# V^T by one transposing DMA in place of TensorE transposes, in the backward pass of attention over a cache

## The chip, the core and the metric

The kernel runs on one core of one Trainium2 chip. The metric is the device time of one execution in microseconds. Three runs of the kernel before gave 5222.84, 5231.35 and 5238.27 us; the median is 5231.35 us.

## What is computed

Forward and backward of a block with two branches on a layer-normalised input xn (2048 rows, 576 columns, bf16): attention with 32 heads of 128 over a K and a V cache of 2048 rows, and a gated branch of width 4608. The output is x + s * silu(B), and the gradients go to x, both caches and all weights.

```
def _A_ref(x, k_cache, v_cache, wq, wo):          # s
    q = (x @ wq) -> [B, H, Sq, Dh]
    scores = einsum("bhqd,bhkd->bhqk", q, k_cache) * Dh ** -0.5
    p = softmax(scores)
    o = einsum("bhqk,bhkd->bhqd", p, v_cache)
    return o.transpose.reshape(B, Sq, H * Dh) @ wo
def _B_ref(x, w_gate, w_up, w_down):
    h = sigmoid(x @ w_gate) * (x @ w_up)
    return h @ w_down
out = x + _A_ref(xn, ...) * silu(_B_ref(xn, ...))
_out, _vjp = jax.vjp(_f, A_x, A_k_cache, A_v_cache, A_wq, A_wo, B_w_gate, B_w_up, B_w_down)
return (_out, *_vjp(grad_out))
```

The backward pass of attention needs, per head, dP = dO V^T. With the head's dimension on the partitions, both factors of this product have to lie in memory as [128 of the head, 2048 rows]; so V, which is loaded in its natural form, has to be transposed once per head.

## The kernel before

The gated branch comes first (lines 165 to 327), then attention (lines 330 to 657), then the weight gradients and the gradient of x (from line 659). The change lies in the attention stage alone.

Attention goes head by head. One head has two halves. In the P half, for each of 16 tiles of 128 query rows, TensorE makes scores (`s_half`, L465), VectorE scales them and tracks the extreme value (L467), and ScalarE takes the exponential of the whole row block, which gives Pq, 128 x 2048 in bf16 (`s_exp`, L476). In the dS half, for each of the same tiles, TensorE makes dP from dO^T and V^T (`dp_half`, L495), and VectorE, with ScalarE's help, turns it into dSq, again 128 x 2048 (L498, L501, L505). Each Pq and nearly each dSq is transposed by a DMA of its own, issued on the SyncE queue (`trans_dma`, L513), into a tile PT or dST; there are 7 such tiles. The dSq of query tile 9 alone is transposed on TensorE, by 16 transposes into PSUM and two copies (`trans_pe`). TensorE then uses PT and V for the output rows and dST and K for dQ (`row_mm`, L525), and Pq with dO and dSq with Q for the gradients of V and K (`kv_mm`, L544).

The tiles K^T, dO by rows, V^T and Q by rows are made with TensorE too: `pe_transposes` (L428 to L432) does 8 transposes into one PSUM accumulator and one copy out of it, and is called twice for each of these tiles. For V^T this is `prep_vt` (L439 to L442): 16 transposes of the natural V tile `Vn`, and two copies on VectorE (L42) into `VT`. Both tiles exist once (`ld1`, one buffer). `load_kv` loads `Kn` and `Vn` on the GpSimd queue, for the next head while the current one runs.

The order of the work is written out by hand. A head is 64 positions long: the P half takes positions 0 to 32 of the head, the dS half 32 to 64. `at(pos, ...)` puts a piece of work at a position; scores and dP are anchors at fixed positions, and everything is emitted in the order of positions. Under `tc.manual_schedule(engines=MAN)` the engines in `MAN` (TensorE, VectorE, ScalarE) execute in exactly this order, while the instructions of SyncE and GpSimd are placed by the scheduler of the framework. The positions that matter here: PT of query tile qt at 2 qt + 2.7, dST at 32 + 2 qt + 2.0, the first use of a group of four PT or dST some 9.4 positions after the first of them, V^T at 22.2 and 24.2. In the last head five loads of output weights (`load_wo`, L374) are written at positions 50 to 62; they fill space that was taken by xnT and dsT and are used in the stage that follows attention.

Of the kernel before, what the change touches and what calls it, by code (L numbers as in the profile page):

```python
# [9 lines left out]
bf = mybir.dt.bfloat16  # L10
# [3 lines left out]
P = 128  # L14
# [81 lines left out]
def kernel(  # L96
# [6 lines left out]
    nc = tc.nc  # L103
    cfg = dict(cfg or {})
    _, S, D = A_x.shape
# [232 lines left out]
    with tc.tile_pool(name="ld2", bufs=2) as ld2, tc.tile_pool(name="ld1q", bufs=1) as ld1q, \  # L338
# [17 lines left out]
        def at(pos, fn, *args):  # L356
            prog.append((pos, len(prog), fn, args))

        def anchor(pos, fn, *args):
            anchors.append((pos, len(anchors), fn, args))  # L360
# [67 lines left out]
        def pe_transposes(src_fn, dst, g, eng):  # L428
            pt = ps_acc.tile([P, 8, P], bf, name="acct", tag="acc")
            for j in range(8):  # L430
                nc.tensor.transpose(pt[:, j, :], src_fn(g * 8 + j), ident[:])  # L431
            alt.copy(dst[:, g * 8:(g + 1) * 8, :], pt[:], eng=eng)  # L432
# [3 lines left out]
                hs.KT = ld1.tile([P, S], bf, name="KT")  # L436
            pe_transposes(lambda j: hs.Kn[:, j, :], hs.KT[:].rearrange("p (t q) -> p t q", q=P), g, eng)

        def prep_vt(hs, g, eng):  # L439
            if g == 0:  # L440
                hs.VT = ld1.tile([P, S], bf, name="VT")
            pe_transposes(lambda j: hs.Vn[:, j, :], hs.VT[:].rearrange("p (t q) -> p t q", q=P), g, eng)  # L442

        def prep_don(hs, g, eng):
            if g == 0:
# [84 lines left out]
        def rows(pos, step, width, hs, T, rhs, g, sinks):  # L530
            bx = Box()
            sink, after = sinks
            for j in range(GQ):
                for kt in range(NT):
                    at(pos + step * j + width * kt / NT, row_mm, bx, hs, T, rhs, g * GQ + j, kt, sink)
            if after:
                at(pos + step * (GQ - 1) + width + AFTER, after)
# [11 lines left out]
        def kv(pos, end, hs, slabs, rhs, half, out_dram):  # L549
            ov = out_dram.rearrange("(p t) d -> p t d", t=NT)  # L550
            bx = Box()
            bx.acc = [None, None]

            def sink(acc, i):
                c = half * 2 + i
                kv_t = stg.tile([P, KPC, P], bf, name="kv")
                alt.copy(kv_t[:], acc[:], eng=KVE[i])
                nc.gpsimd.dma_start(ov[:, c * KPC:(c + 1) * KPC, :], kv_t[:])

            n = 2 * KPC  # L560
            for qt in range(NT):
                for j in range(n):
                    at(pos + (end - pos) * (qt * n + j) / (NT * n), kv_mm, bx, hs, slabs, rhs, half, qt, j, sink)

        def o_sink(hs, g):
            gs = slice(g * GQ, (g + 1) * GQ)
            bx = Box()

            def sink(acc):
                bx.ou = wt.tile([P, GQ, P], bf, name="ou")  # L570
                alt.copy(bx.ou[:], acc[:], eng=OUE)
                bx.prod = wt.tile([P, GQ, P], f32, name="prod", bufs=1)
                nc.gpsimd.tensor_tensor(bx.prod[:], bx.ou[:], hs.dOn[:, gs, :], op=ALU.mult)

            def after():
                prod, ou = bx.prod, bx.ou
                o_n = stg.tile([P, GQ, P], bf, name="o_n", bufs=1)
                nc.vector.tensor_reduce(hs.delta[:, gs], prod[:], axis=AX.X, op=ALU.add)
                nc.gpsimd.tensor_scalar(hs.negdelta[:, gs], hs.delta[:, gs], -1.0, None, op0=ALU.mult)
                nc.gpsimd.tensor_tensor(o_n[:], ou[:], bcast(hs.rinv_all[:, gs], GQ), op=ALU.mult)  # L580
                nc.gpsimd.dma_start(on2_d[g * CH:(g + 1) * CH, hs.h * P:(hs.h + 1) * P].rearrange("(t p) d -> p t d", p=P), o_n[:])

            return sink, after

        def dq_sink(hs, g):
            gs = slice(g * GQ, (g + 1) * GQ)

            def sink(acc):
                dq_n = stg.tile([P, GQ, P], bf, name="dq_n")
                nc.vector.tensor_tensor(dq_n[:], acc[:], bcast(hs.rsc[:, gs], GQ), op=ALU.mult)  # L590
                nc.gpsimd.dma_start(dq2_d[g * CH:(g + 1) * CH, hs.h * P:(hs.h + 1) * P].rearrange("(t p) d -> p t d", p=P), dq_n[:])  # L591

            return sink, None
# [3 lines left out]
        XO, XQ = 12.1, 12.1  # L597
        VA, VB, KA, KB = (22, 38.0), (38.5, 53.5), (58.0, 69.5), (70.5, 82.0)
        QP, DO, KVE, PJE, OUE = (41.0, 3.0), (4.0, 2.5), "ss", "sv", "s"
        KT_AT, DON_AT, VT_AT, QN_AT = (46.3, 2, "v"), (7.2, 5, "v"), (22.2, 2, "v"), (38.3, 2, "s")  # L600
        EXP_AT, RINV_AT, PT_AT, DST_AT, AFTER = 2.1, 4.6, 2.7, 2.0, 3.5
        WO_AT = 50.0
        MAN = {mybir.EngineType.PE, mybir.EngineType.DVE, mybir.EngineType.Activation}
        for h in range(H):
            hs = Head(h)
            b = h * HEAD
            back = lambda x: b - HEAD + x if h else b - 14 + x / 8
            at(back(35.0), load_w, hs)
            at(back(35.1), load_kv, hs)
            for c in range(NCH):  # L610
                at(back(QP[0] + QP[1] * c), proj, hs, "QT", c, PJE[0])
                at(b + DO[0] + DO[1] * c, proj, hs, "dOT", c, PJE[1])
            at(b + DO[0] - 2, prep_wo, hs, "s")
            for g in range(2):
                at(back(KT_AT[0] + KT_AT[1] * g), prep_kt, hs, g, KT_AT[2])
                at(b + DON_AT[0] + DON_AT[1] * g, prep_don, hs, g, DON_AT[2])
                at(b + VT_AT[0] + VT_AT[1] * g, prep_vt, hs, g, VT_AT[2])
                at(b + QN_AT[0] + QN_AT[1] * g, prep_qn, hs, g, QN_AT[2])
            for p in range(NT // 2):
                at(b + 4 * p + 2 + RINV_AT, s_rinv, hs, p)  # L620
                at(b + max(4 * p + 2.1 + RINV_AT, DON_AT[0] + DON_AT[1] * (p // 4) + 0.5), s_scale, hs, p)
            for qt in range(NT):
                p1, p2 = b + 2 * qt, b + H1 + 2 * qt
                for hf in range(NHF):
                    anchor(p1 + hf, s_half, hs, qt, hf)
                    anchor(p2 + hf, dp_half, hs, qt, hf)
                at(p1 + EXP_AT, s_exp, hs, qt)
                if qt in PE_P:
                    for g in range(2):
                        at(p1 + 5.3 + g, trans_pe, hs.PT, hs.P, qt, "PT", g, "s")  # L630
                else:
                    at(p1 + PT_AT, trans_dma, hs.PT, hs.P, qt, "PT")
                if qt in PE_DS:
                    for g in range(2):
                        at(p2 + 4.3 + g, trans_pe, hs.dST, hs.dS, qt, "dST", g, "sv"[g])
                else:
                    at(p2 + DST_AT, trans_dma, hs.dST, hs.dS, qt, "dST")
            for g in range(NG):
                rows(b + 8 * g + XO, 2, 2, hs, hs.PT, "Vn", g, o_sink(hs, g))
                rows(b + H1 + 8 * g + XQ, 2, 2, hs, hs.dST, "Kn", g, dq_sink(hs, g))  # L640
            for half, (pv, pk_) in enumerate(((VA, KA), (VB, KB))):
                kv(b + pv[0], b + pv[1], hs, hs.P, "dOn", half, out_3[0, h])
                kv(b + pk_[0], b + pk_[1], hs, hs.dS, "Qn", half, out_2[0, h])
# [4 lines left out]
                at(bl + WO_AT + 3 * k, load_wo, h0, min(h1, H - 1))  # L648
        prog.sort(key=lambda e: e[:2])
        anchors.sort(key=lambda e: e[:2])  # L650
        with tc.manual_schedule(engines=MAN):
            nxt = 0
            for (pos, _, fn, args) in prog:
                while nxt < len(anchors) and anchors[nxt][0] <= pos:
                    anchors[nxt][2](*anchors[nxt][3])
                    nxt += 1
                fn(*args)

    OB = 5
    if True:  # L660
# [19 lines left out]
        with tc.tile_pool(name="c1b", bufs=1, side="right", reuse_waits="tile") as blk, \  # L680
# [3 lines left out]
                tc.tile_pool(name="c1pt", bufs=2, space=PSUM) as pst, \  # L684
                tc.manual_schedule(engines=MAN | {mybir.EngineType.SP, mybir.EngineType.Pool}):
            gins = {}
# [188 lines left out]
        with tc.tile_pool(name="c4c", bufs=1, reuse_waits="tile") as chp, tc.tile_pool(name="c4s", bufs=2, reuse_waits="tile") as sb, \  # L875
# [10 lines left out]
            for sbi in range(S // SB2):  # L886
# [20 lines left out]
                for sl in range(nsl):  # L907
# [17 lines left out]
                    t = sb.tile([P, D], f32, name="t")  # L925
# [38 lines left out]
```

## Time and profile before

| what | value |
|---|---|
| median of three runs | 5231.35 us |
| span of the profiled execution | 5231.1 us |
| heads | 32, the first scores at 517.3 us, the last head from 3640.0 us |
| transposing DMAs of PT, dST | 512 and 480, median landing 5.7 and 6.2 us after the issue |
| transposes of V on TensorE | 512, median 219 ns |
| copies into VT on VectorE | 64, median 686 ns |
| bytes on SyncE's DMA queue in one head (1562.2 to 1663.4 us) | 16.85 MB |
| bytes on GpSimd's DMA queue in the same stretch | 3.44 MB |

The profile is of one execution. The profiler gives the span from the first to the last instruction, and no other time of that execution; the span is 0.25 us below the median of the runs. Busy times are per engine; TensorE's matmuls overlap each other, so that the busy time of a group is less than the count times the mean. The granted TensorE clock is full in every head. SyncE only issues DMAs, so its rows show the length of the issuing instruction, which includes the wait for a semaphore and for a place in the queue. In a row of the waits the name in front waited, and the name behind the arrow ended the wait.

### The profile page before, as it was taken

The page shows a single profiled execution, that of the slowest core. Times are in us where ns is not written, and L with a number is a line of the kernel's source. Part 1 is how long each engine was busy: PE and PEld are TensorE (multiplying, and loading weights), DVE is VectorE, ACT ScalarE, POOL GpSimd, SP SyncE. Part 2 cuts the span into 40 slices and gives each one's busy share as a digit, 9 for nine tenths or more (in the row PEclk, how much of TensorE's full clock was granted, in tenths as well). Part 3 has the DMA queues.
Part 4 walks back from the last instruction along what each step waited for, and adds up shares of the span by engine and source line. Part 5 has one row for each costly group of instructions (what it writes and reads, how often), then busy time and mean ns, then how long its engine had stood idle before and what let it go on. Part 6 is the DMA issues. An engine that isn't in the chain of part 4 may idle for free.

```text
span 5231.1 us, 128038 instructions
## 1 busy us (share of the span) xinstructions
PE 5100.0 (97%) x55184; PEld 3649.0 (70%) x55184; DVE 3262.9 (62%) x5108; ACT 2290.1 (44%) x2931; POOL 1444.3 (28%) x2102
## 2 busy tenths in 40 slices
PE   8999999999999999999999999999899999999999
PEld 3444777777777777777777777777657788744454
DVE  4545888888888888888888888888532222210111
ACT  6531665565566556556556655655301221100000
POOL 2222233233233323323323332332222222211000
PEclk9999999999999999999999999999999999999999
DMA  7489999999999999999999999999999556686765
GB/s 274 183 205 166 190 192 199 193 197 194 193 197 198 198 198 199 199 197 195 197 202 198 194 201 199 197 197 201 204 223 227 174 169 185 200 232 152 162 146 124
DMA packets 2712232, 1013.46 MB, mean 194 GB/s; under 512 B 2525296, under 2 KB 2645872, under 8 KB 2711664
## 3 DMA queue, kind: packets, MB, share of 16 engines
q1 hardware_dynamic: 2628256, 726.57, 80.8%
q0 software_dynamic: 83408, 278.71, 17.9%
q8 instruction: 431, 7.06, 0.6%
q14 instruction: 137, 1.12, 0.1%
HBM read 172.54 MB, written 201.00 MB: 71 GB/s over the span
## 4 chain that ended last, share of the span: by engine, by line
PE 81%; issue 6%; DVE 6%; DMA 5%; POOL 1%; SPq 1%; ACT 0%; DVEq 0%; POOLq 0%; ACTq 0%
PE acckv L544 15%; PE acc L525 14%; PE dp L495 8%; PE acc L905 7%; PE sp L465 6%; PE accw L807 6%; DVE sneg L467 4%; PE accp L424 4%; PE dh L781 3%; PE acc L306 3%; PE accd L795 3%; PE accq L863 3%; PE acc L854 2%; PE acct L431 2%; PE acc L723 2%
## 5 line engine op out<-in xcount | busy, mean ns | idle before, releaser
L476 ACT ACTIVATE Pq<-sneg,nm 128x2048 bf16<-128x2048 bf16 x512 | 1024.5, 2001 | 389.2 <-DVE sneg L467 386.1
L525 PE MATMUL acc<-Kn,dST 128*128 128x128 bf16 x8192 | 1066.6, 219 | 22.5 <-DMA dST<-dSq 22.4
L525 PE MATMUL acc<-Vn,PT 128*128 128x128 bf16 x8192 | 1022.4, 219 | 10.7 <-DMA PT<-Pq 10.7
L544 PE MATMUL acckv<-dOn,Pq 128*128 128x128 bf16 x8192 | 1031.7, 219 | 0.0
L498 DVE SCALAR_TENSOR_TENSOR dSq<-dp,delta,Pq 128x1024 bf16<-128x1024 f32 x608 | 773.6, 1281 | 349.9 <-PE dp L495 347.6
L544 PE MATMUL acckv<-Qn,dSq 128*128 128x128 bf16 x8192 | 896.2, 219 | 0.0
L544 PEld LDWEIGHTS <-Pq 128*128 128x128 bf16 x8192 | 793.3, 98 | 117.1 <-issue 0.3
L525 PEld LDWEIGHTS <-PT 128*128 128x128 bf16 x8192 | 765.8, 98 | 153.2 <-DMA PT<-Pq 14.2
L525 PEld LDWEIGHTS <-dST 128*128 128x128 bf16 x8192 | 759.0, 98 | 158.1 <-DMA dST<-dSq 28.8
L544 PEld LDWEIGHTS <-dSq 128*128 128x128 bf16 x8192 | 719.0, 98 | 99.8 <-issue 0.3
L467 DVE TENSOR_SCALAR_CACHE_REDUCE sneg<-sp,nm 128x1024 bf16<-128x1024 f32 x512 | 656.5, 1282 | 82.0 <-PE sp L465 56.5
L467 DVE TENSOR_SCALAR_CACHE_REDUCE sneg<-sp 128x1024 bf16<-128x1024 f32 x512 | 625.0, 1221 | 59.5 <-PE sp L465 51.2
L501 ACT ACTIVATE t<-dp,negdelta 128x1024 bf16<-128x1024 f32 x416 | 463.6, 1114 | 420.1 <-PE dp L495 363.2
L465 PE MATMUL sp<-KT,QT 128*128 128x512 bf16 x2048 | 609.2, 379 | 32.5 <-DVE sneg L467 25.4
L495 PE MATMUL dp<-VT,dOT 128*128 128x512 bf16 x2048 | 609.5, 379 | 0.3 <-DVE dSq L498 0.3
L484 POOL TENSOR_TENSOR dOn<-dOn,rinv_all 128x256 bf16<-128x256 bf16 x256 | 155.9, 609 | 658.0 <-DVE rinv_all L480 540.9
L505 DVE TENSOR_TENSOR dSq<-t,Pq 128x1024 bf16<-128x1024 bf16 x416 | 319.0, 767 | 0.0
L807 PEld LDWEIGHTS <-xn_all 128*128 128x128 bf16 (+1 forms) x2880 | 282.7, 100 | 38.6 <-issue 11.1
L905 PEld LDWEIGHTS <-cf 128*128 128x128 bf16 x2304 | 146.0, 98 | 141.7 <-DMA cf<-dg_d 3.6
L918 DVE SCALAR_TENSOR_TENSOR junk<-dxn,xn_all 128x576 f32<-128x576 f32 x16 | 12.1, 758 | 370.3 <-ACT dxn L913 370.3
L591 POOL DMA_DIRECT2D dq_d<-dq_n x128 | 98.6, 770 | 471.9 <-DVE dq_n L590 463.5
L465 PEld LDWEIGHTS <-QT 128*128 128x128 bf16 x2048 | 163.3, 98 | 53.1 <-issue 51.7
(173 smaller groups left out, 6956.1 us busy)
## 6 DMA issues: line engine op xcount, KB each, us to landing
out_dram<-kv POOLq DMA_DIRECT2D x256, 128.0 KB, 4.8
h_d<-h_row POOLq DMA_DIRECT2D x48, 384.0 KB, 2.7
a_d<-a_row POOLq DMA_DIRECT2D x48, 384.0 KB, 2.6
b_d<-b_row POOLq DMA_DIRECT2D x48, 384.0 KB, 3.2
a_blk<-a_d SPq DMA_DIRECT2D x18, 1024.0 KB, 5.8
b_blk<-b_d SPq DMA_DIRECT2D x18, 1024.0 KB, 21.3
du_d<-du_blk POOLq DMA_DIRECT2D x18, 1024.0 KB, 8.5
dg_d<-dg_blk POOLq DMA_DIRECT2D x18, 1024.0 KB, 11.5
```

The costliest lines, as they stand in the source:

```text
L424: nc.tensor.matmul(acc[:], lhsT=w[:, i, :], rhs=srcT[:, i, cs], start=(i == 0), stop=False)
L465: nc.tensor.matmul(sp[:, c * CH:(c + 1) * CH], lhsT=hs.QT[:, qs], rhs=hs.KT[:, hf * HW_ + c * CH: hf * HW_ + (c + 1) * CH], start=True, st ...
L467: nc.vector.tensor_scalar(sneg[:, hf * HW_:(hf + 1) * HW_], sp[:], -SCALE, None if hf == 0 else nm[:, hf - 1:hf], op0=ALU.mult, op1=ALU.mi ...
L476: nc.scalar.activation(Pq[:], sneg[:], AF.Exp, bias=nm[:, hf:hf + 1], scale=-1.0, accum_out=hs.rs_all[:, qt:qt + 1])
L495: nc.tensor.matmul(dp[:, c * CH:(c + 1) * CH], lhsT=hs.dOT[:, qs], rhs=hs.VT[:, hf * HW_ + c * CH: hf * HW_ + (c + 1) * CH], start=True, s ...
L498: nc.vector.scalar_tensor_tensor(dSq[:, hsl], dp[:], hs.delta[:, qt:qt + 1], Pq[:, hsl], op0=ALU.subtract, op1=ALU.mult)
L501: nc.scalar.activation(t[:], dp[:], AF.Identity, bias=hs.negdelta[:, qt:qt + 1], scale=1.0)
L505: nc.vector.tensor_tensor(dSq[:, hsl], t[:], Pq[:, hsl], op=ALU.mult)
L525: nc.tensor.matmul(bx.acc[:, j, :], lhsT=T[qt][:, kt, :], rhs=getattr(hs, rhs)[:, kt, :], start=(kt == 0), stop=(kt == NT - 1))
L544: nc.tensor.matmul(bx.acc[i][:, jj, :], lhsT=slabs[qt][:, k0:k0 + P], rhs=getattr(hs, rhs)[:, qt, :], start=(qt == 0 and jj == 0), stop=(q ...
L807: nc.tensor.matmul(acc[:kd, :FB], lhsT=xn_all[:, st, d0:d0 + kd], rhs=blk_[:, st, :], start=(st == 0), stop=(st == NT - 1))
L905: nc.tensor.matmul(accs[sl][j][:, :nn], lhsT=ch[:, kk, sl * P:(sl + 1) * P], rhs=w_[:, n0:n0 + nn], start=(pi == 0 and kk == 0), stop=(las ...
```

## The change

`prep_vt`, called twice per head at positions 22.2 and 24.2, is replaced by `turn`, called once per head at position 5.6. It takes the whole `Vn` tile, 128 x 2048 in bf16, and writes `VT` by one transposing DMA on SyncE's queue. The 16 transposes on TensorE, the two PSUM accumulators and the two copies on VectorE are gone. In addition, SyncE is put among the engines that execute in the written order, for this stage. GpSimd's instructions are still placed by the scheduler.

```diff
-        def prep_vt(hs, g, eng):
-            if g == 0:
-                hs.VT = ld1.tile([P, S], bf, name="VT")
-            pe_transposes(lambda j: hs.Vn[:, j, :], hs.VT[:].rearrange("p (t q) -> p t q", q=P), g, eng)
+        def turn(hs, name, src):
+            t_ = ld1.tile([P, S], bf, name=name)
+            setattr(hs, name, t_)
+            nc.sync.dma_start_transpose(t_[:].rearrange("p (t q) -> p t q", q=P), src(hs).rearrange("p t d -> p (t d)"))
...
-        KT_AT, DON_AT, VT_AT, QN_AT = (46.3, 2, "v"), (7.2, 5, "v"), (22.2, 2, "v"), (38.3, 2, "s")
+        KT_AT, DON_AT, VT_AT, QN_AT = (46.3, 2, "v"), (7.2, 5, "v"), 5.6, (38.3, 2, "s")
...
+        MANH = MAN | {mybir.EngineType.SP}
...
+            at(b + VT_AT, turn, hs, "VT", lambda hs: hs.Vn[:])
             for g in range(2):
...
-                at(b + VT_AT[0] + VT_AT[1] * g, prep_vt, hs, g, VT_AT[2])
...
-        with tc.manual_schedule(engines=MAN):
+        with tc.manual_schedule(engines=MANH):
```

## The prediction

> **What bounds the kernel now.** The change touches only the attention stage, so I first looked for that stage on the page, in its slices and engine sums.
>
> ```profile
> PE 5100.0 (97%) x55184; PEld 3649.0 (70%) x55184; DVE 3262.9 (62%) x5108; ACT 2290.1 (44%) x2931; POOL 1444.3 (28%) x2102
> ...
> PE   8999999999999999999999999999899999999999
> ...
> DMA  7489999999999999999999999999999556686765
> ```
>
> Attention is slices 5 to 29 (the first L465 matmul starts at 517 us, the last head at 3640 us): 32 heads. TensorE and the DMA engines both stand at 9 throughout, so two resources are full together, and the change takes from one and gives to the other. The question is which one has room.
>
> TensorE first. From the matmul records, the distance between the first L465 matmuls of neighbouring heads is 100.32 us, to 0.03, in 15 of 31 heads and 100.73 us in the mean (95.5 to 105.4). A number that repeats to the hundredth is the pace of an instruction stream, not of transfers; the other heads lie above it. The waits of PE between 650 and 3600 us say why:
>
> ```profile
> PE sp L465 <- DVE sneg L467: 19.5, 58, 0.4
> PE acc L525 <- DMA dST<-dSq: 12.1, 14, 1.6
> ```
>
> (Total us, times, longest.) In 29 heads PE lost 12 us to late dS transposes. Small, but these are already arriving too late now and then. So next the SyncE queue, which issues all transposes, over two heads:
>
> ```profile
> 1538.01 52.05 SPq L513 DMA_TRANSPOSE PT<-Pq  x16
> 1590.17 48.91 SPq L513 DMA_TRANSPOSE dST<-dSq  x15
> 1639.16 50.47 SPq L513 DMA_TRANSPOSE PT<-Pq  x16
> 1689.74 50.23 SPq L513 DMA_TRANSPOSE dST<-dSq  x15
> ```
>
> (Start, length.) Each row ends within 0.12 us of the next one's start: 31 transposes fill a whole head, about 3.2 us each. Is the queue waiting for its sources, or are they waiting for it? One pair answers, the sixth dSq of that head and its transpose:
>
> ```profile
> 1600.01 0.68 DVE L505 TENSOR_TENSOR dSq<-t,Pq 128x1024 bf16<-128x1024 bf16 x1
> ...
> 1609.06 1.73 SPq L513 DMA_TRANSPOSE dST<-dSq  x1
> ```
>
> The source was done at 1600.7, its transpose was issued 8.4 us later. Doing this for every transpose of heads 2 to 30 (issue against the end of the ACT or DVE instruction that finishes its source), the sources wait 3.5 to 8 us in the dS half and 0.1 to 3.3 us in the P half; SyncE waits for a source for only 1.58 us per head, nearly all before the sixth to ninth PT. So the transpose path is occupied 100.73 - 1.58 = **99.15 us of 100.73**. PE paces most heads, with a DMA path 1.6% below its limit right behind it.
>
> **The change, part by part.**
>
> *Removed on PE:* 16 transposes per head. Their price is what they hold back on the weight-load row, not the 219 ns each on the group's line, since they overlap:
>
> ```profile
> 1567.48 0.49 PEld L431 LDWEIGHTS <-Vn 128*128 128x128 bf16 x8
> 1567.92 0.10 PEld L525 LDWEIGHTS <-PT 128*128 128x128 bf16 x1
> ```
>
> Eight take 0.44 us from start to the next start, 16 take 0.89 us, so 28 us over 32 heads. *Removed on DVE:* two copies:
>
> ```profile
> L42 DVE COPY VT<-acct 128x1024 bf16<-128x1024 bf16 x64 | 43.9, 686 | 4.7 <-PE acct L431 4.7
> ```
>
> 2 x 0.686 = 1.37 us per head. Both copies (1569.4 and 1573.0 in that head) lie in the stretch 1563 to 1575 where the chain of waits runs through L467 on DVE and PE idles, so here the copies, and not the transposes, are what the end would feel: a gain of 1.37 us per head, 44 us in all, if nothing else is late; at least the 28 us of PE. Two PSUM accumulators per head also come free; I cost that at nothing, because the one wait of PE for an accumulator in the list of waits (acct behind dq_n, 6.5 us in 29 heads) is 0.2 us per head.
>
> *Added on the DMA path:* one 128x2048 bf16 transpose per head, the same shape as PT. No row shows a VT transpose; the bounds come from its 991 sisters. Taking the landings in order, the 302 intervals in which no other queue moved anything have a lower quartile of 1.68 us and a mean of 2.08. A least-squares fit of all intervals (bytes of SyncE's queue, bytes of GpSimd's queue, instruction loads) gives 2.44 us per transpose, and with it 75 us for transposes, 11 us for GpSimd's 3.4 MB and 14 us for 11.5 instruction loads of 16 KB, together 100 us of a head. The mean occupation, 99.15 / 31 = 3.2 us, carries a share of that other traffic and is the upper end; 1.68 is the lower. I take 2.44, the fit, because the queue is backlogged where this transpose enters it. 32 fewer TensorE instruction pairs save an eighth of an instruction load, about 0.15 us.
>
> [...] The trace's 512 KB in 2.44 us are 215 GB/s, and its fast quarter 310 GB/s.
>
> *What else the new DMA does.* Position 5.6 puts it between the second and third PT. There SyncE is 3 us behind. VT is free (the last dp of the head before ended at least 13 us earlier) and Vn landed at least 37 us earlier, so the instruction adds no wait of its own; if it did, every PT behind it would be late. PT from the third on moves back by up to 2.4 us. Their reserves (landing to first use by L525, medians) are 9 us there and 2.3 to 5 us from the tenth on, and the 1.58 us of idle lies between, so the P half mostly absorbs it. The dS half inherits the rest; its reserve is 0.6 us at the eighth and 1.1 at the ninth dST. That is what will be late next.
>
> *SyncE in written order.* The transposes already issue in the written order in every head (16 PT, 15 dST), so nothing moves there. Only the five output-weight loads of L374 move: today they go out between 3630 and 3678 us, under the last head's P half, which takes 58.28 us where others take 51.40, 6.9 us lost; written, they go at positions 50 to 62, between the last dST. Their 4.57 MB are 16 to 21 us of DMA at 290 to 215 GB/s. So 6.9 us come back, and between nothing and 21 us are paid at the last dST: -7 to +14 us; I take +2, as the last dST already keep PE waiting.
>
> *Sum.* DMA per head: 99.15 + 2.44 - 0.15 = 101.44 us, plus 0.3 us of idle that remains because the reserve varies from head to head: 101.74 against 100.73, **+1.0 us**. PE would now allow 98.95 to 99.4, so its gain is not felt. Over 31 periods +31 us, with the loads +33: 5231.1 + 33 = **5264 us**. The profiled span, 5231.1, lies 0.25 us from the median of the runs, so no correction. With 1.68 us per transpose the head would be 100.7 to 101.0 (5229 to 5240); with 3.2 us, 102.5 (5231 + 55 + up to 14 = 5300).
>
> **Rivals.**
>
> *The DMA path has more room than its queue shows* (faster). A queue that is always full can hide slack: SyncE may be held only by a limit on descriptors in flight, and if the engines behind it take an extra transpose without delaying the others, PE and DVE decide, and the gain is 28 to 44 us: 5203 to 5187. For it: half the heads run at PE's exact pace in spite of the backlog. Against it: all six heads longer than 101 us (105.4 at the worst) have at most 0.8 us of SyncE idle; a path with room would not lengthen them. It decides if the marginal transpose costs under about 1 us, beneath the 5% point of 1.53 us.
>
> *A transpose costs the fast quarter or less* (no change). [...] For it: the intervals below 1.7 us. Against it: they follow a stall, when descriptors have piled up. [...]
>
> *The idle cannot be used* (slower still). If the 1.58 us lie where PT's source is late whatever the queue does, and the new DMA costs its full 3.2 us, a head costs +3.1 us: 5231 + 96 = 5327.
>
> *The change does not do what it says:* VT could be held by Vn or by the old VT. With 13 and 37 us in hand I give that nothing of its own.
>
> **Chances and range.** This kernel's measurement can tell about 0.3% (16 us) from no change. Forecast (slower, 5246 to 5300): 0.57. More room: 0.23, faster. No change: 0.16. Idle unusable: 0.04, slower. So faster 0.23, same 0.16, slower 0.61. The range reaches from the lower end of the faster rival, 5187, to the forecast's upper bound, 5300; the forecast's own is 5246 to 5300.
>
> **What would show it.** Right: the head's period no longer repeats at one value and lies near 101.7 us; PE's waits on dST grow from 12 us to over 40 us; SyncE's idle goes from 1.6 us per head towards 0.3; DVE's busy time falls by 44 us without shortening the span. Wrong: a period fixed at or below 99.4 us with dST waits as before (DMA had room), or VT's landing delayed by its own waits.

## The result and the profile after

The changed kernel is slower: 5298.39 us median (5278.81 to 5323.32, 4 runs) against 5234.81 us for the kernel before beside it, ratio 1.0112 (95% interval 1.0064 to 1.0160). On another chip with six runs of it the median was 5305.95 us and the ratio 1.0130 (1.0101 to 1.0160). The profiled execution took 5323.32 us, the longest of its four, with a span of 5321.5 us; a second profile had 5294.9 us.

The first lines of the page look almost as they did before the change; PE and the DMA engines stand at 9 again:

```profile
PE 5101.7 (96%) x54672; PEld 3627.1 (68%) x54672; DVE 3228.3 (61%) x5044; ACT 2292.4 (43%) x2931; POOL 1447.9 (27%) x2102
...
PE   8999999999999999999999999999898999999999
...
DMA  7587999999999999999999999999999665596865
```

What changed is who ends PE's waits. The waits of PE between 650 and 3600 us (total us, times, longest):

```profile
PE acc L525 <- DMA dST<-dSq: 48.3, 39, 3.3
PE acc L525 <- DMA PT<-Pq: 43.2, 53, 2.4
PE sp L465 <- DVE sneg L467: 14.3, 49, 0.7
```

dST rose from 12.1 to 48.3 us, PT from 1.7 to 43.2. Accordingly the chain that ended last now runs through transfers for 15% of the span instead of 5%. First the kernel before, then the changed one:

```profile
PE 81%; issue 6%; DVE 6%; DMA 5%; POOL 1%; SPq 1%; ACT 0%; DVEq 0%; POOLq 0%; ACTq 0%
```

```profile
PE 71%; DMA 15%; issue 5%; DVE 5%; SPq 2%; POOL 1%; ACT 1%; DVEq 0%; POOLq 0%; ACTq 0%
```

The SyncE queue, from one head's PT to the next one's (start, length):

```profile
1550.25 6.70 SPq L513 DMA_TRANSPOSE PT<-Pq  x2
1557.00 3.02 SPq L442 DMA_TRANSPOSE VT<-Vn  x1
1560.12 43.34 SPq L513 DMA_TRANSPOSE PT<-Pq  x14
1603.57 49.49 SPq L513 DMA_TRANSPOSE dST<-dSq  x15
1653.15 6.25 SPq L513 DMA_TRANSPOSE PT<-Pq  x2
```

VT goes out where it was written, without a wait (its median landing is 5.1 us, PT's was 5.7), and again there is no hole: SyncE's idle for want of a source fell from 1.58 to 0.03 us per head. 103 us lie between the first and the last row instead of 101.

Measured as the distance between the first L467 instructions of neighbouring heads (complete in all profiles), the mean period went from 100.74 to 103.27 us, 103.14 in the second profile; no value is shared by more than two heads any more, where 15 of 31 had been 100.32 us. Over 31 periods that is +78 us (+74). The rest of the first profile's +90 us is -7 us before the first head and +20 us behind attention, which the second profile does not have (its stages behind attention are within 8 us of before), so this rest is one execution's own.

Now the number that explains the period. These are the DMA lines of 29 heads (from the third head's start to the last one's), first before, then after:

```profile
DMA packets 1902964, 577.01 MB, mean 197 GB/s; under 512 B 1877062, under 2 KB 1878518, under 8 KB 1902582
```

```profile
DMA packets 1964958, 591.66 MB, mean 197 GB/s; under 512 B 1940084, under 2 KB 1940516, under 8 KB 1964580
```

14.65 MB more, 0.505 MB per head, at the same 197 GB/s: 2.6 us per head. (The new DMA is 0.524 MB per head. The difference is mainly a load of output weights of 1.18 MB, which lies in the window of the kernel before and, under the written order, behind it in the changed one.) The rate did not rise to take the added work.

### The profile page after: what moved, and what is told of

It reads as the page before. It is cut to its first block, busy times and chain, and to the rows that moved or that the text cites. A ratio compares the mean times of both kernels' runs of the same rounds, so it can differ in the third digit from the quotient of the medians.

```text
span 5321.5 us, 127041 instructions
## 1 busy us (share of the span) xinstructions
PE 5101.7 (96%) x54672; PEld 3627.1 (68%) x54672; DVE 3228.3 (61%) x5044; ACT 2292.4 (43%) x2931; POOL 1447.9 (27%) x2102
## 4 chain that ended last, share of the span: by engine, by line
PE 71%; DMA 15%; issue 5%; DVE 5%; SPq 2%; POOL 1%; ACT 1%; DVEq 0%; POOLq 0%; ACTq 0%
PE acckv L544 13%; PE acc L525 12%; PE acc L906 7%; DMA PT<-Pq 7%; DMA dST<-dSq 6%; PE sp L465 5%; PE dp L495 5%; PE accw L808 5%; DVE sneg L467 4%; PE accp L424 4%; PE acc L306 3%; PE accq L864 3%; PE dh L782 3%; PE acc L855 2%; PE accd L796 2%
## 5 line engine op out<-in xcount | busy, mean ns | idle before, releaser
L467 DVE TENSOR_SCALAR_CACHE_REDUCE sneg<-sp,nm 128x1024 bf16<-128x1024 f32 x512 | 657.3, 1284 | 93.2 <-PE sp L465 62.4
L467 DVE TENSOR_SCALAR_CACHE_REDUCE sneg<-sp 128x1024 bf16<-128x1024 f32 x512 | 625.0, 1221 | 60.3 <-PE sp L465 51.3
L919 DVE SCALAR_TENSOR_TENSOR junk<-dxn,xn_all 128x576 f32<-128x576 f32 x16 | 12.1, 758 | 370.4 <-ACT dxn L914 370.4
```

The lines of the kernel that those rows point to most:

```text
L467: nc.vector.tensor_scalar(sneg[:, hf * HW_:(hf + 1) * HW_], sp[:], -SCALE, None if hf == 0 else nm[:, hf - 1:hf], op0=ALU.mult, op1=ALU.mi ...
```

## The experiments

Theory D: in attention the 16 DMA engines carry a fixed rate of this mix of traffic, 197 to 198 GB/s, and carried it already before; a head lasts as long as its bytes take, unless TensorE's stream is longer. Against it: O, the written order costs; P, TensorE's relief is felt beside the DMA's price; Q, the place of the DMA costs; R, the DMA path has room; S, the price is an issue on SyncE, not bytes. "Floor" below is the shortest period that several heads share. It is read as TensorE's own pace, because most heads share it (22 of 31) in the run where PE hardly waits for transposes (7.9 us in 29 heads), and no more than two share a period in the changed kernel, where it waits 91.5 us. Periods are of one profile each, and kernels with the same work differ in the mean by some tenths of a us between profiles; ratios are of the timed runs, always against the kernel before.

**The order alone**, on the kernel before:

```diff
+        MANH = MAN | {mybir.EngineType.SP}
-        with tc.manual_schedule(engines=MAN):
+        with tc.manual_schedule(engines=MANH):
```

> The kernel before with SyncE in the written order and nothing else. Theory D (the DMA engines carry about 195 GB/s in attention, before and after, so a head lasts as long as its bytes, and the added transpose costs 512 KB at that rate): head periods as before, 100.3 to 100.8 us; only the five late weight loads and the first loads of the stage behind attention move, +5 to +15 us in all, that is 5236 to 5250 us. Theory O (the written order of SyncE is what costs): most of the 58 us, 5280 us or more.

Ratio 0.9995 (0.9977 to 1.0012), mean period 100.81, floor 100.32 in 15 heads, as before. Attention's last head came out 5 us shorter; the 5 to 15 us that D expected from the late loads did not appear. O is out.

**The DMA alone**: the same, and V's DMA at 5.6 into VT, with `prep_vt` kept, writing the same values over it.

```diff
+            at(b + 5.6, turn, hs, "VT", lambda hs: hs.Vn[:])
```

> The kernel before with SyncE in the written order and the new DMA of V at position 5.6 added, while the TensorE transposes and the copies stay and write the same values over it. Theory D: the head is paced by its DMA bytes as after the change, so the time is that of the changed kernel, 5280 to 5325 us, head period near 103 us. Theory P (the time lost is the DMA's, but TensorE's relief gives part of it back): 28 to 44 us above the changed kernel, 5325 us or more.

5314.18 us, ratio 1.0139 (1.0118 to 1.0159), mean period 103.55: the DMA alone brings the whole loss. The same kernel and the changed one, side by side on one chip:

> The changed kernel once more, to stand beside the kernel with the DMA added and the TensorE transposes kept on the same chip. Theory D: 5290 to 5325 us. Theory P: 28 us or more below that other kernel.

> The kernel before with SyncE in the written order and the DMA of V added, TensorE transposes and copies kept, once more. Theory D: within 15 us of the changed kernel on the same chip. Theory P: 28 to 44 us above it.

Changed kernel 5305.95 us, ratio 1.0130 (1.0101 to 1.0160); with the TensorE work kept 5320.82 us, 1.0157 (1.0121 to 1.0193). They are 15 us apart, with overlapping intervals; on the first two chips the ratios, 1.0139 and 1.0112, lie as far apart. P's 28 to 44 us do not appear, but the runs are too few to say whether none of TensorE's relief is felt, as D has it, or a part.

**Neither the DMA nor the transposes**: the changed kernel with V^T of head 0 for all heads.

```diff
-                                 rhs=hs.VT[:, hf * HW_ + c * CH: hf * HW_ + (c + 1) * CH], start=True, stop=True)
+                                 rhs=hs0.VT[:, hf * HW_ + c * CH: hf * HW_ + (c + 1) * CH], start=True, stop=True)
...
-            at(b + VT_AT, turn, hs, "VT", lambda hs: hs.Vn[:])
+            if h == 0:
+                at(b + VT_AT, turn, hs, "VT", lambda hs: hs.Vn[:])
+                hs0 = hs
```

> The changed kernel with V^T made for head 0 alone and used for all heads (leaves out the transposes of V of the other 31 heads): neither the TensorE transposes nor the DMA. Theory D: 31 transposes per head on the DMA as before, so the period stays at 99.5 to 100.5 us and loses its fixed value, 5190 to 5240 us with the late loads. Theory R (the DMA path has room, TensorE and VectorE pace): fixed period of 98.9 to 99.4 us, 5195 us or less.

Ratio 0.9974 (0.9954 to 0.9994). This is the run that shows the limit. The floor fell to 99.48 us, but only 9 heads are at it and the mean is 100.61, 0.13 below before. PE's waits:

```profile
PE acc L525 <- DMA dST<-dSq: 25.6, 26, 4.7
PE sp L465 <- DVE sneg L467: 15.9, 58, 0.4
```

Its 29 heads:

```profile
DMA packets 1904741, 576.48 MB, mean 198 GB/s; under 512 B 1879867, under 2 KB 1880299, under 8 KB 1904363
```

TensorE was given 0.84 us per head, and the mean period of this profile fell by 0.13; the wait for dST doubled from 12.1. The timed runs gave a little more: the median, 5224.62 us, is 15 us below the kernel before and 10 below the run of the order alone, where 31 x 0.84 would be 26 us. So 31 transposes alone already took the DMA engines about 100.6 us, at 198 GB/s. R, which expected 5195 us or less, is out. D's expected mean of 99.5 to 100.5 was missed by 0.1; its time was met. Against this run the changed kernel moves 15.18 MB more in the 29 heads, 0.523 MB per head, which is the new DMA. At 197 GB/s these bytes take 2.65 us; the heads are 2.66 us longer in the mean of all 31 periods and 2.87 in the mean of these 29.

**The copies alone**: the kernel before with the written order, the TensorE transposes of V kept, the copies left out for heads 1 to 31.

```diff
         def prep_vt(hs, g, eng):
+            if hs.h:
+                pt = ps_acc.tile([P, 8, P], bf, name="acct", tag="acc")
+                for j in range(8):
+                    nc.tensor.transpose(pt[:, j, :], hs.Vn[:, g * 8 + j, :], ident[:])
+                hs.VT = Head.VT
+                return
             if g == 0:
-                hs.VT = ld1.tile([P, S], bf, name="VT")
+                hs.VT = Head.VT = ld1.tile([P, S], bf, name="VT")
```

> The kernel before with SyncE in the written order; the TensorE transposes of V stay, their two VectorE copies per head are left out for heads 1 to 31, which use V^T of head 0 (so V^T is wrong for them). Without both, the shortest head period was 99.48 us against 100.32. If the copies were the price, as the prediction said, the shortest period falls to 99.5 us or below here too. If the transposes were, it stays near 100.3 us and the time near that of the kernel before, 5225 to 5245 us.

Floor 99.86 in 12 heads, mean 100.92, ratio 0.9991 (0.9969 to 1.0013). The floor lies between the two expectations: copies 0.46, transposes the other 0.38 of the 0.84 us. The mean does not follow the floor down here either.

**Back to 31 transposes**: the changed kernel with one more dS on TensorE.

```diff
-    PE_DS = {9}
+    PE_DS = {3, 9}
```

> The changed kernel with dS of query tile 3 transposed on TensorE as that of tile 9 is, so that the DMA again carries 31 transposes per head and TensorE again 80 transposes. Theory D: back to the time before, plus the cost of the late loads: 5230 to 5250 us, period 100.3 to 101 us. Theory Q (it is the place of the new DMA ahead of the PT, not the amount, that costs): PE still waits for PT as in the changed kernel, over 5270 us.

Ratio 1.0032 (1.0016 to 1.0048), floor 101.04 in 14 heads, mean 101.33: a fixed pace is back, and the list of waits has no dST left:

```profile
PE sp L465 <- DVE sneg L467: 15.9, 58, 0.4
PE acc L525 <- DMA PT<-Pq: 9.0, 18, 1.3
PE accp L424 <- ACT ou L40: 7.0, 29, 0.2
```

The new DMA is still ahead of the PT, yet they are late by 9 us instead of 43. For these waits the amount decides, not the place. The 0.3% that is left is TensorE's: a dS there costs 101.04 - 99.48 = 1.56 us per head. The median, 5260 us, is 10 above what D expected, and the period is above its 100.3 to 101 us: D had set TensorE's price too low.

**Half the bytes**: blocks 0 to 7 of V by DMA, 8 to 15 by TensorE.

```diff
+            nc.sync.dma_start_transpose(hs.VT[:, :S // 2].rearrange("p (t q) -> p t q", q=P), hs.Vn[:, :NT // 2, :].rearrange("p t d -> p (t d)"))
...
-                at(b + VT_AT[0] + VT_AT[1] * g, prep_vt, hs, g, VT_AT[2])
+                if g == 1:
+                    at(b + VT_AT[0] + VT_AT[1] * g, prep_vt, hs, g, VT_AT[2])
```

> The kernel before with SyncE in the written order, where the first 8 of the 16 blocks of V are transposed by a DMA of half the size at position 5.6 and the other 8 by TensorE as before. Theory D: half of the added DMA, so about half of the loss: mean period 101.6 to 102.2 us, 5260 to 5290 us. Theory S (the cost is one per DMA, an issue of SyncE, not its bytes): the whole loss, 5300 us.

Ratio 1.0055 (1.0026 to 1.0085), mean period 101.67, against 100.74 with none and 103.27 with all. Half the bytes, 37% of the loss by the period and between 40 and 50% by the ratios (1.0055 against 1.0112 and 1.0130); S, which expected the whole, fails. Its 29 heads:

```profile
DMA packets 1935373, 584.12 MB, mean 198 GB/s; under 512 B 1910497, under 2 KB 1910929, under 8 KB 1934993
```

**Another place**: the changed kernel with the DMA of V behind the ninth PT.

```diff
-        KT_AT, DON_AT, VT_AT, QN_AT = (46.3, 2, "v"), (7.2, 5, "v"), 5.6, (38.3, 2, "s")
+        KT_AT, DON_AT, VT_AT, QN_AT = (46.3, 2, "v"), (7.2, 5, "v"), 19.6, (38.3, 2, "s")
```

> The changed kernel with the DMA of V at position 19.6 instead of 5.6, behind the ninth PT instead of the second. Theory D (the amount on the DMA engines costs, not the place): within 10 us of the changed kernel, 5285 to 5320 us, mean head period 102.5 to 103.5 us. Theory Q (the PT behind the new DMA come late and that costs): clearly less lost in the P half, 5270 us or less.

5337.20 us, 17 above the range D gave; ratio 1.0165 (1.0110 to 1.0220), mean period 103.58. The mean period is 0.08 above D's range too. Not better, so Q fails; the waits are of the changed kernel's size, and PE waits for none of the first nine PT, but for the later ones:

```profile
PE acc L525 <- DMA dST<-dSq: 52.5, 43, 4.4
PE acc L525 <- DMA PT<-Pq: 46.3, 57, 2.6
```

**Without the order**: the changed kernel under `MAN`.

```diff
-        with tc.manual_schedule(engines=MANH):
+        with tc.manual_schedule(engines=MAN):
```

> The changed kernel without the written order of SyncE; the DMA of V then stands in the queue just ahead of the last dST of the head before, where it has to wait for the last dP that reads the old VT. Theory D: as the changed kernel, 5285 to 5320 us, or up to 20 us more for that wait; theory O is out after the run of the order alone and would expect 5240 us here.

5311.63 us, ratio 1.0111 (1.0046 to 1.0176), mean period 103.12: a third place in the queue, the same loss as in the first. The kernel with the DMA behind the ninth PT took 26 us more on the same chip, with four runs of each; that the place costs something besides the amount is not excluded.

**Less of another queue's traffic**: the changed kernel, where only head 0 stores its gradients of V and K.

```diff
-                nc.gpsimd.dma_start(ov[:, c * KPC:(c + 1) * KPC, :], kv_t[:])
+                if hs.h == 0:
+                    nc.gpsimd.dma_start(ov[:, c * KPC:(c + 1) * KPC, :], kv_t[:])
```

> The changed kernel without the stores of the gradients of V and K for heads 1 to 31 (leaves those outputs out, 1.05 MB per head on GpSimd's queue; the products and the copies stay). Theory D (all queues share the 16 DMA engines): the head's bytes fall from 20.4 to 19.4 MB, below the kernel before, so TensorE paces: period 99.5 us in most heads, about 5200 us. Theory S (SyncE's queue alone is the limit, whatever GpSimd moves): mean period stays near 103 us, over 5280 us.

Ratio 0.9889 (0.9838 to 0.9941), 5190.94 us; floor 99.48 us in 22 heads, mean 99.68. SyncE issues the same 32 transposes per head as in the changed kernel, and PE hardly waits for one:

```profile
PE acc L525 <- DMA PT<-Pq: 5.8, 7, 1.6
PE acc L525 <- DMA dST<-dSq: 2.1, 2, 1.0
```

SyncE's queue (q1) moved the same bytes in 29 heads, in 3000.3 us in the changed kernel and in 2893.6 us here:

```profile
q1 hardware_dynamic: 1930404, 486.70, 101.5%
q1 hardware_dynamic: 1931411, 486.96, 104.6%
```

So neither SyncE's queue nor transposing by itself is the limit, but something that the transposes share with GpSimd's transfers. D calls it the DMA engines; whether it is the engines themselves or a path to memory that they share, these runs do not tell apart. In bytes per head and mean period, the kernels read: 19.36 MB 99.68 us (TensorE's floor), 19.88 MB 100.61 (without V^T work), 20.14 MB 101.67, 20.40 MB 103.1 to 103.6. In bytes, all but the first differ by transposes alone; that a byte of GpSimd's costs as much is not shown, since the first is at TensorE's floor.

By these prices no step of this kind beats the kernel before: with 31 transposes the DMA limit (100.6) and TensorE's floor (100.32) lie 0.3% apart, a step towards DMA costs 2.5 us per head and gives back 0.84, a step towards TensorE costs 1.56.

## Why the prediction was right, and where it failed

*What bounds the kernel*: right that two resources are full; the DMA side was fuller than it said, 0.1% below the measured period (100.61 of 100.74) and not 1.6%. *The sign and its mechanism*: right, TensorE's relief is real (the floor falls from 100.32 to 99.48) and the DMA engines take back more. *The price of the transpose*: 2.44 us by the fit; measured 2.4 to 2.5 us per head against the kernel before, 2.7 to 2.9 against the one without V^T work. Right to some tenths.

*The sum* is where it failed: +1.0 us per head was forecast, +2.4 to +2.5 came, and +64 us in all instead of +33. The step is "the transpose path is occupied 100.73 - 1.58 = 99.15 us", which let the new DMA fill 1.58 us of SyncE's idle. The shortfall is that idle almost exactly. The idle was filled, as the prediction said (1.58 to 0.03 us per head), and it bought nothing, because it was not idle of the engines: in the kernel before a transpose lands 2.8 us (median of 992) after SyncE has finished issuing it, and at the end of an issue one or two, never more, have still to land, so the engines go on working through such a gap. Heads 2 to 30 (counted from 0) have there 33 gaps of more than 0.5 us, 40 us together; in them the DMA engines moved 204 GB/s, and 194 GB/s in the 5 us from the start of each, against 197 in the mean. One of the two longest gaps: SyncE's waits between 2755 and 2770 us (the longest, 3.5 us, is this gap), and the engines in it (the last number is GB/s):

```profile
SPq L513 <- ACT Pq L476: 6.5, 3, 3.5
2761.88:2765.32 3.44, 3.44 (x53) 2.97 (x52) 2.94 (x6) 2.00 (x2) 0.35 (x1) 1.00 1.14 210
```

The kernel without both shows how much room there really was: with TensorE's floor at 99.48 the heads took 100.61, so against 100.74 the DMA had 0.1 us in this profile (0.3 to 0.5 by the timed runs, if all that they gained lies in the heads), not 1.58. The rival "the idle cannot be used" had the outcome and not the mechanism: by its condition the idle would have stayed, while SyncE's idle went and the period grew all the same. Its price was too high (3.2 where 2.44 was due); with 2.44, less 0.15, it would have said 5231 + 31 x 2.3 = 5302 us.

*The range* was met partly by luck. The median, 5298.39 us, lies 1.6 us below its upper end of 5300; two of the four executions, and the median on the other chip, lie above. The upper end reached that far because 3.2 us per transpose and 14 us for the late loads, both more than came, made up for an idle that was not there to use.

*The signs*: dST waits over 40 us (48.3) and SyncE's idle towards nothing (0.03) came, and so did the end of the fixed period, at 103.2 us in place of 101.7. DVE's busy time fell by 34.6 us, not 44.

*The copies would be felt, not the transposes, 1.37 us*: wrong in size and in kind. Copies 0.46, transposes 0.38. What holds the floor at 99.48 us beyond that was not taken apart.

*The P half mostly absorbs it*: wrong. PE's waits for PT rose by 41.5 us, those for dST by 36.2. *Late loads, +2 us between -7 and +14*: within its range, near the lower end; the last head came out 5 us shorter, and the order alone changed nothing that the timed runs can tell. (The granted clock, 1.00 in the heads ahead of it, was 0.83 in the last head of the kernel before from 3740 to 3750 us.) *No wait of VT itself*: right. *32 fewer instruction pairs*: 16 pairs, which are 32 instructions; the page counts 427 instruction loads of 16 KB on q8 where it counted 431, an eighth of one per head, and the 0.15 us estimated for it is too small to matter.

*A transpose at the fast quarter or less* (no change): out. The fast quarter is 1.68 us; the new DMA cost 2.4 to 2.9 us per head. Half a transpose at that price is 0.84 us, an estimate from the quartile of the landing intervals and less than the 1.58 us of idle that the prediction let it fill, and the half-size run should have lost nothing. That run lost 0.9 us per head, at 198 GB/s for all queues together, where the kernel before has 197.

## What to carry to other kernels

Here two resources were full, and moving work between them cost what the fuller one charged, 2.4 to 2.9 us per head; of the 0.84 us gained on the side that was relieved, 0.1 to 0.5 came through even without the DMA, because the other side already set the mean. Where both look full, take the work away from both sides once: the period that is left (100.61 us here, above a floor of 99.48) shows the second limit. Here a queue that waited before it issued did not show that the engines behind it were free: they moved 204 GB/s in its gaps, against 197 in the mean. So divide the bytes of the stage by its time, and see whether any variant gets a higher rate.

## What the runs showed that I had not expected

The rate of the mixed traffic over 29 heads is 197 to 198 GB/s in the four kernels that wait for transfers and whose bytes stand above (before, changed, without V^T work, half the bytes), from 31 to 32 transposes per head. With the new one in another place the estimate is the same: 20.40 MB, the changed kernel's bytes per head, over periods of 103.58 and 103.12 us are 197 and 198 GB/s. In the two that TensorE paces it is lower, 196 and 194. Executions of the changed kernel differ by more than 40 us (5278.81 to 5323.32), though those of the kernel before do so too (5222.84 to 5265.43); single heads of the changed kernel's profile, the first left out, last from 100.3 to 110.1 us with the same work. Moving a dS transpose from DMA to TensorE costs 1.56 us per head, though 16 transposes (those of V in the kernel before) hold TensorE for only 0.89; where the rest comes from is not shown.
